# Fixed places for the plain matrix products of a fused attention and feed-forward kernel

## The chip, the core and the metric

The kernel runs on one core of a Trainium2 chip. A core has TensorE (matrix products, "PE" in the profile; its weight loads are "PEld"), VectorE ("DVE"), ScalarE ("ACT"), GpSimd ("POOL") and SyncE ("SP"), each with a queue of instructions of its own that it works through in order, and 16 DMA engines. Matrix products read SBUF and write PSUM. The metric is the time of one execution on the device in microseconds, lower is better.

## The reference

Inputs q, k, v have shape [8, 8, 576, 64]. Two attentions are added: a coarse one on means over groups of four tokens (144 by 144 scores), whose output is repeated four times, and a local one over a band of seven tokens. The sum, laid out as x of 4608 tokens by 512, goes through an RMS norm and a gated feed-forward layer of width 1536.

```python
def sm_attn(qq, kk, vv):                       # softmax(scale * qq kk^T) vv
q_d = q.reshape(B, H, S // 4, 4, D).mean(axis=3)       # k_d, v_d alike
out_up = np.repeat(sm_attn(q_d, k_d, v_d), 4, axis=2)
mask = np.abs(pos[:, None] - pos[None, :]) < 4         # local attention
x = (out_up + out_local) -> [4608, 512]
xn = x / np.sqrt(mean(x * x) + 1e-6) * rms_g
g, val = xn @ w_gate, xn @ w_val
out = (g / (1 + np.exp(-g)) * val) @ w_out
```

## The kernel before

**Chunks.** The tokens are worked in 18 chunks of 256, in two halves (`j`) of 128 partitions. A chunk's feed-forward layer has six inner tiles (`n` from 0 to 5), each of 256 columns of the inner width. Every product of this layer is made of three products of half-wide numbers in the type fp32r, because x, the weights and the inner values are each split into a high and a low part (`xh`, `xl`; `hs` holds both parts of the inner value).

- The *first products* (L1388, `ps_h<-xh,w` and `ps_h<-xl,w`, 128x256) are 24 for the gate and 24 for the value of an inner tile, 48 in all.
- Between them and the second products lie ScalarE's tanh (L1396, into `sil`), VectorE's gate step (L1399), VectorE's product with the value (L1404), ScalarE's high part (L1410, into `hs`) and VectorE's low part (L1413, into `hs`). "Gate or value steps" are L1399 and L1404, "an hs" is L1413.
- The *second products* (L1427, `ps_o<-wo,hs`, 128x512) are twelve for an inner tile. They are emitted one inner tile late (`LAG = 1`), behind the first products of the next inner tile, so that the second products of a chunk's last inner tile fall into the next chunk. `hs` has two buffers. Every third of the twelve reads the low part.

**Plain products.** Everything else on TensorE is in plain fp32 and writes one of three PSUM buffers named `ps_a`:

- for the coarse attention of two heads (one `Coarse` object, a "pair"): four products of scores (L593, "s"), then peaks and a scale on VectorE (L599, L608) and four exponentials on ScalarE (L613, into `a_g`), eight transposes of `a_g` ("turns", L623), two copies on ScalarE (L703), and eight products with the values (L638, "v"; each leaves two records in the trace, as the products of scores do), a scale into `o_g` on VectorE and a store to DRAM. The sums over four tokens that these need are made of loads by SP and POOL and additions (class `Sums`, L417);
- for a chunk's x: one product that sums the squares (L1010, "mean") and eight transposes of x (L1033, "x transposes"), after which ScalarE copies the high part xh (L1037) and VectorE subtracts to the low part xl (L1041).

**Local attention.** It is VectorE's and ScalarE's work, for the chunk that follows the one in the feed-forward layer: eight steps of score products (L917, `prod`, about 1 us each) and score sums (L921), a softmax, eight steps of value products (L970 on VectorE, L963 on ScalarE, a share on POOL) and value sums (L980 into `x_t`), two adds of the coarse output (L993), squares on ScalarE (L1003), the root of the norm, two scalings (L1020). The tile `x_t` has a limited number of buffers, so that the sums for one chunk wait until the x transposes of the chunk before have read the old contents.

**What sets the order.** Chunks 0 to 2, and the attention of the first chunks, are placed by a planner with a table of due times; the change leaves it alone. Chunks 3 to 17 run in a loop (L1571 to L1600). For each chunk it holds a list `todo` of pairs (time in half inner tiles, what to emit) for the next chunk: local attention, mean and x transposes from `Attention.steps`, and two pairs of heads from `Coarse.steps`. After each half inner tile it emits what is due:

```python
todo = nxt.steps(9.1 if c == FIRST else 6.5)
...
at = 1.2 + 2.5 * i
todo += zip((at + 0.1, at + 1.3), Coarse(*it).steps(lambda: fwd.last))
```

A scheduler of the language then orders what was emitted for each engine by its own estimate of when each instruction is ready; `tc.issue_after(x)` keeps an instruction behind `x` on its engine. Before the change only the products of scores (behind the last first product so far, `fwd.last`) and one first product of chunk 3 are pinned in this way. Twenty pairs of heads are done in this loop, two in each of the chunks 3 to 12; chunks 13 to 16 have only a mean and x transposes, chunk 17 nothing.

## Time and profile before

| what | value |
| --- | --- |
| median of 3 runs | 1089.92 us (1088.96 to 1090.8) |
| profiled execution | 1089.94 us, its span in the trace 1088.1 us |
| TensorE busy | 1066.7 us, 98% |
| TensorE weight loads busy | 970.2 us, 89% |
| VectorE busy | 909.6 us, 84% |
| ScalarE busy | 598.6 us, 55% |
| GpSimd busy | 160.8 us, 15% |

The span is the time from the first to the last record of the profiled execution; the rest of its time lies around it. Busy shares are averages over stages with different limits. The ends of matrix products in the trace are modelled, so where a product begins is read from its own start and where it ends from the start of the next one. A line of the timeline that joins several instructions ("x12") gives the start of the first.

### The profile page before, as it was taken

Reading aid. Unit: us, or ns where it says so; the run is one execution under the profiler, and the core shown is the slowest. Engines: PE = TensorE matmul, PEld = TensorE weight load, DVE = VectorE, ACT = ScalarE, POOL = GpSimd, SP = SyncE. Lnnn points to the kernel's source line nnn. Section 1 sums busy time; section 2 is a strip of 40 time slices with the busy share of each in tenths; the row PEclk is TensorE's granted clock in tenths of the full one; section 3 lists DMA queues with packets and bytes.
Section 4 is the critical chain, followed back from the end, with each engine's and each line's share of the span. In section 5 each row is a group of like instructions: output and inputs, shape, how many; then the busy total and the mean of one; then the engine's idle time right before and its main releaser. Section 6 shows DMA issues by size and latency. Waiting matters only on the chain.

```text
span 1088.1 us, 21642 instructions
## 1 busy us (share of the span) xinstructions
PE 1066.7 (98%) x7983; PEld 970.2 (89%) x7983; DVE 909.6 (84%) x1554; ACT 598.6 (55%) x2029; POOL 160.8 (15%) x200
## 2 busy tenths in 40 slices
PE   7899999999999999999999999999999999999997
PEld 4569899899989999999999999999999999999996
DVE  7799999798969897979797979798998898986421
ACT  4686565737266565656564737383737373645111
POOL 6544564300210101010101010100000000000000
PEclk9899999999999999999999999999999999999999
DMA  9885657333654535353525253522221222210000
GB/s 292 274 237 167 182 134 155 77 91 86 132 102 117 118 99 102 107 106 87 126 85 128 68 130 86 132 77 82 63 86 54 79 78 74 80 40 20 1 20 20
DMA packets 79182, 114.09 MB, mean 105 GB/s; under 512 B 33038, under 2 KB 40406, under 8 KB 79076
## 3 DMA queue, kind: packets, MB, share of 16 engines
q1 hardware_dynamic: 48308, 88.40, 26.3%
q0 software_dynamic: 11680, 19.78, 11.6%
q10 hardware_dynamic: 19088, 4.53, 1.9%
q8 instruction: 62, 1.02, 0.4%
q14 instruction: 44, 0.36, 0.1%
HBM read 100.86 MB, written 11.80 MB: 104 GB/s over the span
## 4 chain that ended last, share of the span: by engine, by line
PE 85%; DVE 6%; DMA 3%; issue 2%; POOL 2%; ACT 1%; SPq 1%; DVEq 0%; POOLq 0%; ACTq 0%
PE ps_h L1388 51%; PE ps_o L1427 25%; PE ps_a L638 3%; DMA w<-in_w_val_dram 1%; PE ps_a L593 1%; PE ps_a L623 1%; DVE prod L917 1%; PE ps_a L1033 1%; DVE x_t L980 1%; DVE sc L921 1%; PE ps_a L1258 1%; DVE sil L1404 0%; POOL hs L1413 0%; DMA vs<-in_v_sum_dram 0%; DMA wo<-in_w_val_dram 0%
## 5 line engine op out<-in xcount | busy, mean ns | idle before, releaser
L1388 PE MATMUL ps_h<-xh,w 128*128 128x256 f32 x3456 | 632.6, 281 | 0.0
L1388 PEld LDWEIGHTS ps_h<-xh,w 128*128 128x128 f32 x3456 | 537.6, 188 | 9.7 <-issue 3.1
L1388 PE MATMUL ps_h<-xl,w 128*128 128x256 f32 x1728 | 482.5, 280 | 0.0
L1427 PE MATMUL ps_o<-wo,hs 128*128 128x512 f32 x1296 | 327.1, 396 | 4.2 <-POOL hs L1413 1.7
L1388 PEld LDWEIGHTS ps_h<-xl,w 128*128 128x128 f32 x1728 | 325.2, 188 | 5.8 <-issue 2.0
L963 ACT ACTIVATE prod<-kv,sc 128x64 f32<-128x64 f32 x1024 | 261.9, 406 | 28.9 <-DVE sc L954 15.5
L1427 PEld LDWEIGHTS ps_o<-wo,hs 128*128 128x128 f32 x1296 | 232.8, 188 | 49.1 <-DVE hs L1413 2.8
L980 DVE TENSOR_REDUCE x_t<-prod 128x128 f32<-128x896 f32 x128 | 134.5, 1080 | 39.5 <-PE ps_a L1033 36.8
L1410 ACT ACTIVATE hs<-sil 128x512 fp32r<-128x512 f32 x108 | 68.2, 631 | 165.5 <-DVE sil L1404 140.1
L1396 ACT ACTIVATE sil<-ps_h 128x512 f32<-128x512 f32 x108 | 64.1, 595 | 148.7 <-PE ps_h L1388 140.8
L917 DVE TENSOR_TENSOR prod<-q_t,kv 128x896 f32<-128x896 f32 x128 | 138.6, 1089 | 0.2
L921 DVE TENSOR_REDUCE sc<-prod 128x14 f32<-128x896 f32 x128 | 136.9, 1075 | 0.2
L1399 DVE SCALAR_TENSOR_TENSOR sil<-sil,ps_h 128x512 f32<-128x512 f32 x108 | 73.7, 683 | 52.1 <-ACT sil L1396 52.1
L970 DVE TENSOR_TENSOR prod<-sc,kv 128x384 f32<-128x384 f32 (+1 forms) x128 | 105.9, 868 | 0.1
L1404 DVE SCALAR_TENSOR_TENSOR sil<-sil,ps_h 128x512 f32<-128x512 f32 x108 | 73.9, 684 | 22.6 <-PE ps_h L1388 22.1
L417 POOL DMA_DIRECT2D qk<-in_qk_sum_dram x42 | 39.0, 928 | 340.0 <-DMA qk<-in_qk_sum_dram 282.1
L1413 DVE TENSOR_TENSOR hs<-sil,hs 128x512 fp32r<-128x512 f32 x102 | 69.9, 685 | 17.9 <-ACT hs L1410 17.8
L613 ACT ACTIVATE a_g<-ps_a,m_g 72x144 f32<-72x144 f32 x128 | 46.5, 370 | 54.2 <-DVE m_g L608 50.0
L417 POOL DMA_DIRECT2D vs<-in_v_sum_dram x42 | 39.4, 937 | 104.1 <-DMA vs<-in_v_sum_dram 80.7
L1003 ACT ACTIVATE up_t<-x_t 128x128 f32<-128x128 f32 x128 | 39.1, 305 | 18.3 <-DVE x_t L993 12.2
L638 PEld LDWEIGHTS ps_a<-vs,a_g 72*72 72x72 f32 x512 | 39.2, 150 | 7.4 <-ACT a_g L613 2.9
L638 PE MATMUL ps_a<-vs,a_g 72*72 72x64 f32 x512 | 40.8, 234 | 5.1 <-ACT a_g L613 2.7
(154 smaller groups left out, 808.0 us busy)
## 6 DMA issues: line engine op xcount, KB each, us to landing
kv<-in_k_pad_dram SPq DMA_DIRECT2D x56, 320.0 KB
kv<-in_v_pad_dram SPq DMA_DIRECT2D x56, 320.0 KB
qk<-in_qk_sum_dram POOLq DMA_DIRECT2D x42, 288.0 KB, 4.5
out_dram<-o_sb SPq DMA_DIRECT2D x96, 72.0 KB
vs<-in_v_sum_dram POOLq DMA_DIRECT2D x42, 144.0 KB, 4.3
q_t<-in_q_band_dram SPq DMA_DIRECT2D x150, 36.0 KB
w<-in_w_gate_dram SPq DMA_DIRECT2D x8, 512.0 KB
w<-in_w_val_dram SPq DMA_DIRECT2D x8, 512.0 KB
```

The lines of the kernel that those rows point to most:

```text
L417: nc.gpsimd.dma_start(out=t, in_=(qk_sum, v_sum)[i][self.b, j, :, self.half], accum_op=ALU.add)
L638: nc.tensor.matmul(out=op[:, par, c], lhsT=at[:, kc, c * HALF:(c + 1) * HALF], rhs=self.sums.vs[:, 2 * (self.hp % 2) + par, kc], start=(kc ...
L917: nc.vector.tensor_tensor(out=pr, in0=bcast(q[:, s0:s0 + 2], 2, NO), in1=window(k, s0), op=ALU.mult)
L921: nc.vector.tensor_reduce(out=self.sc[:, j, par, s0:s0 + 2], in_=self.pr[i], axis=AX.X, op=ALU.add,)
L963: nc.scalar.activation(out=self.pr[i][:, o, s], in_=self.v[j, par][:, s0 + s + o], func=AF.Copy, scale=p[:, s, o:o + 1],)
L970: (nc.vector if engine == "DVE" else nc.gpsimd).tensor_tensor(out=self.pr[i][:, a:b], in0=bcast(p[:, :, a:b].rearrange("p s o -> p o s"), ...
L980: nc.vector.tensor_reduce(out=self.x[j][:, s0:s0 + 2, par], in_=pr.rearrange("p o s d -> p s d o"), axis=AX.X, op=ALU.add,)
L1388: self.last = nc.tensor.matmul(out=p[n][:, i], lhsT=wi[:, k], rhs=xi[:, k], start=(m == 0), stop=(m == 3 * KT - 1),).ins
L1399: nc.vector.scalar_tensor_tensor(out=self.sil[n], in0=self.sil[n], scalar=1.0, in1=self.g[n], op0=ALU.add, op1=ALU.mult,)
L1404: nc.vector.scalar_tensor_tensor(out=self.sil[n], in0=self.sil[n], scalar=0.5, in1=self.v[n], op0=ALU.mult, op1=ALU.mult,)
L1413: (nc.gpsimd if engine == "POOL" else nc.vector).tensor_tensor(out=self.hs[n][:, 1], in0=self.sil[n], in1=self.hs[n][:, 0], op=ALU.subtract,)
L1427: nc.tensor.matmul(out=self.o[j], lhsT=lhs[:, cols], rhs=rhs, start=(f == 0 and m == 0), stop=(f == NF - 1 and m == 2),)
```

## The change

In chunks 4 to 17 the plain products of the next chunk and of the coarse attention no longer come from `todo`. Each chunk has `slots`: lists of what to emit in inner tile `n`, behind its 48 first products and ahead of the twelve second products of inner tile `n - 1`. `in_line` chains these plain products and the second products behind one another on TensorE, beginning behind the last first product, and the next gate's first product is put behind the last of them. The slots are:

- 0: values of the second pair of the chunk before, scores of the first pair;
- 2: turns of the first pair, and the next chunk's mean with what follows it up to the norm;
- 3: values of the first pair, scores of the second;
- 4: the x transposes of the next chunk, with xh and xl;
- 5: turns of the second pair.

A pair's two turns are now emitted ahead of its two copies. The value steps of local attention are emitted 0.25 apart in place of 0.42, the adds at 4.1 and 4.9 in place of 4.8 and 6.4, and the loads of the next pair's sums in the chunk ahead, at 9.0 (`sum_up`). Chunk 3 keeps its `todo` list, without slots; its last second products fall into chunk 4 and are placed there.

```diff
@@ -508,6 +508,16 @@
     whole_og = {}
+    line = {"last": None}
+
+    def in_line(make):
+
+        with tc.issue_after(line["last"]) if line["last"] else nullcontext():
+            done = make()
+        if line["last"]:
+            line["last"] = done.ins
+        return done
+
     class Coarse:
@@ -538,6 +548,32 @@
                 self.store()
             return low, high
+
+        def sum_up(self):
+            if (self.b, self.hp // 2) not in sums:
+                sums[self.b, self.hp // 2] = Sums(self.b, self.hp // 2)
+            self.sums = sums[self.b, self.hp // 2]
+
+        def emit_scores(self):
+            self.sum_up()
+            self.scores()
+            self.peak(0)
+            self.peak(1)
+            self.scale()
+            self.powers(0)
+            self.powers(1)
+
+        def emit_turns(self):
+            self.invert()
+            for par in range(2):
+                self.turn(par)
+            for par in range(2):
+                self.copy(par)
+
+        def emit_values(self):
+            self.values()
+            self.scaled()
+            self.store()
         def plan(self, at, after=()):
             b, hp, tag = self.b, self.hp, self.tag
...
@@ -787,9 +823,19 @@
                 self.low(j)
             todo = [(0.37 * i, lambda i=i: score(i)) for i in range(8)] + [(3.0, softmax)]
-            todo += [(3.1 + 0.42 * i, lambda i=i: value(i)) for i in range(8)]
-            todo += [(at, lambda j=j: add(j)) for j, at in enumerate((4.8, 6.4))]
+            todo += [(3.1 + (0.42 if mean_at else 0.25) * i, lambda i=i: value(i)) for i in range(8)]
+            todo += [(at, lambda j=j: add(j)) for j, at in enumerate((4.8, 6.4) if mean_at else (4.1, 4.9))]
+            if mean_at is None:
+                self.emit_root = root
+                return todo
             return todo + [(mean_at, root), (10.4, lambda: turn(0)), (10.5, lambda: turn(1))]
+
+        def emit_x(self):
+            for j in range(2):
+                self.turn(j)
+            for j in range(2):
+                self.high(j)
+                self.low(j)
         def plan(self):
             c, np_, T = self.c, self.np, due[self.c]
...
@@ -1424,10 +1470,10 @@
             for j in range(2):
                 cols = slice(j * P, (j + 1) * P)
                 for m, (lhs, rhs) in enumerate(((hh, w[0]), (hh, w[1]), (hl, w[0]))):
-                    nc.tensor.matmul(
+                    in_line(lambda: nc.tensor.matmul(
                         out=self.o[j], lhsT=lhs[:, cols], rhs=rhs,
                         start=(f == 0 and m == 0), stop=(f == NF - 1 and m == 2),
-                    )
+                    ))
         def copy(self, j):
             if j == 0:
...
@@ -1568,25 +1614,48 @@
-    att, late = atts[FIRST], []
+    att, late, ahead, behind = atts[FIRST], [], [], None
     for c in range(FIRST, NCH):
-        todo = []
-        if c + 1 < NCH:
+        todo, slots = [], {}
+        n = min(2, len(coarse) - done)
+        pairs = [Coarse(*it) for it in coarse[done:done + n]]
+        done += n
+        if c == FIRST:
             nxt = Attention(c + 1, 4, 0)
-            todo = nxt.steps(9.1 if c == FIRST else 6.5)
-            n = min(2, len(coarse) - done)
-            for i, it in enumerate(coarse[done:done + n]):
+            todo = nxt.steps(9.1)
+            for i, it in enumerate(pairs):
                 at = 1.2 + 2.5 * i
-                todo += zip((at + 0.1, at + 1.3), Coarse(*it).steps(lambda: fwd.last))
-            done += n
-            todo.sort(key=lambda t: t[0])
+                todo += zip((at + 0.1, at + 1.3), it.steps(lambda: fwd.last))
+        else:
+            if behind:
+                slots[0] = [behind.emit_values]
+            behind = None
+            if pairs:
+                a, behind = pairs
+                slots.setdefault(0, []).append(a.emit_scores)
+                slots[2] = [a.emit_turns]
+                slots[3] = [a.emit_values, behind.emit_scores]
+                slots[5] = [behind.emit_turns]
+            if c + 1 < NCH:
+                nxt = Attention(c + 1, 4, 0)
+                todo = nxt.steps(None)
+                slots.setdefault(2, []).append(nxt.emit_root)
+                slots[4] = [nxt.emit_x]
+        if done < len(coarse):
+            todo.append((9.0, Coarse(*coarse[done]).sum_up))
+        todo.sort(key=lambda t: t[0])
         fwd = Forward(att)
         for n in range(NF // 2):
             for half in range(2):
-                if c == FIRST and half == 0 and n == NF // 2 - 1:
-                    fwd.behind = nxt.meant
+                if half == 0:
+                    fwd.behind = nxt.meant if c == FIRST and n == NF // 2 - 1 else line["last"]
+                    line["last"] = None
                 (fwd.emit_value if half else fwd.emit_gate)(n)
                 if half:
+                    if c > FIRST:
+                        line["last"] = fwd.last
+                    for emit in slots.get(n, []):
+                        emit()
                     late.append((fwd, n))
                     if len(late) > LAG:
                         fw, g = late.pop(0)
```

The pieces left out put `in_line` around the products of scores, turns, values, the mean and the x transposes, in the same way.

What moves is shown at three places. The names are those of the program; the numbers in them tell buffers and parts of weights apart.

The first place is TensorE in the third inner tile of a chunk with coarse work: the end of its first products, the turns of a pair, and the second products behind them. Before:

```order
L1388 MATMUL ps_h<-xl_5939,w_1_805 128x256
L623 MATMUL ps_a<-ident_sb,a_g 72x72
L1388 MATMUL ps_h<-xh_5938,w_1_806 128x256
L1388 MATMUL ps_h<-xh_5938,w_1_805 128x256
L1388 MATMUL ps_h<-xl_5939,w_1_805 128x256
L623 MATMUL ps_a<-ident_sb,a_g 72x72 x4
L1427 MATMUL ps_o<-wo_0_549,hs 128x512 x2
L623 MATMUL ps_a<-ident_sb,a_g 72x72 x3
L1427 MATMUL ps_o<-wo_0_549,hs 128x512
L1427 MATMUL ps_o<-wo_0_550,hs 128x512
```

After:

```order
L1434 MATMUL ps_h<-xl_4393,w_1_805 128x256
L1434 MATMUL ps_h<-xh_4392,w_1_806 128x256
L659 MATMUL ps_a<-ident_sb,a_g 72x72 x8
L1056 MATMUL ps_a<-ss,same_sb 128x8
L1473 MATMUL ps_o<-wo_0_549,hs 128x512
L1473 MATMUL ps_o<-wo_0_550,hs 128x512
L1473 MATMUL ps_o<-wo_0_549,hs 128x512 x2
```

The eight turns stood in three pieces among first and second products; now they stand in one piece, with the mean behind them, and only second products follow.

The second place is TensorE where chunk 3 ends and chunk 4 begins: the x transposes of chunk 4, its first first products, and the second products of chunk 3's last inner tile. Before:

```order
L1033 MATMUL ps_a<-ident_sb,x_t 128x128 x8
L1427 MATMUL ps_o<-wo_2_1329,hs 128x512
L1427 MATMUL ps_o<-wo_2_1330,hs 128x512
L1427 MATMUL ps_o<-wo_2_1329,hs 128x512
L1427 MATMUL ps_o<-wo_2_1330,hs 128x512
L1388 MATMUL ps_h<-xh_3717,w_0_359 128x256 x3
L1427 MATMUL ps_o<-wo_2_1329,hs 128x512 x3
L1427 MATMUL ps_o<-wo_2_1330,hs 128x512
L1427 MATMUL ps_o<-wo_2_1329,hs 128x512 x2
L1427 MATMUL ps_o<-wo_2_1330,hs 128x512
L1427 MATMUL ps_o<-wo_2_1329,hs 128x512
L1388 MATMUL ps_h<-xl_3718,w_0_359 128x256
```

After, in two pieces, between which stand the rest of the 48 first products:

```order
L1434 MATMUL ps_h<-xh_2882,w_2_906 128x256
L1079 MATMUL ps_a<-ident_sb,x_t 128x128 x8
L1434 MATMUL ps_h<-xh_3727,w_0_359 128x256 x2
L1434 MATMUL ps_h<-xl_3728,w_0_359 128x256
L1434 MATMUL ps_h<-xh_3727,w_0_360 128x256
L1434 MATMUL ps_h<-xh_3727,w_0_359 128x256
```

```order
L1434 MATMUL ps_h<-xl_3728,w_0_359 128x256
L1434 MATMUL ps_h<-xh_3727,w_0_360 128x256
L629 MATMUL ps_a<-qk 72x144 x4
L1473 MATMUL ps_o<-wo_2_1329,hs 128x512
L1473 MATMUL ps_o<-wo_2_1330,hs 128x512
L1473 MATMUL ps_o<-wo_2_1329,hs 128x512 x2
```

The twelve second products stood in front of the first product that reads xl; now they stand behind all 48 first products of chunk 4's first inner tile, with the products of scores ahead of them.

The third place is VectorE in chunk 13, from the second to the third hs after the x transposes. Before:

```order
L1413 TENSOR_TENSOR hs<-sil,hs 128x512
L1399 SCALAR_TENSOR_TENSOR sil<-sil,ps_h 128x512
L917 TENSOR_TENSOR prod<-q_t,kv 128x896
L921 TENSOR_REDUCE sc<-prod 128x14
L1404 SCALAR_TENSOR_TENSOR sil<-sil,ps_h 128x512
L921 TENSOR_REDUCE sc<-prod 128x14
L917 TENSOR_TENSOR prod<-q_t,kv 128x896
L1399 SCALAR_TENSOR_TENSOR sil<-sil,ps_h 128x512
L1413 TENSOR_TENSOR hs<-sil,hs 128x512
```

After:

```order
L1459 TENSOR_TENSOR hs<-sil,hs 128x512
L963 TENSOR_TENSOR prod<-q_t,kv 128x896
L1026 TENSOR_REDUCE x_t<-prod 128x2x64
L967 TENSOR_REDUCE sc<-prod 128x14
L1445 SCALAR_TENSOR_TENSOR sil<-sil,ps_h 128x512
L1039 TENSOR_TENSOR x_t<-x_t,up_t 128x512
L963 TENSOR_TENSOR prod<-q_t,kv 128x896 x2
L1450 SCALAR_TENSOR_TENSOR sil<-sil,ps_h 128x512
L967 TENSOR_REDUCE sc<-prod 128x14 x2
L1445 SCALAR_TENSOR_TENSOR sil<-sil,ps_h 128x512
L963 TENSOR_TENSOR prod<-q_t,kv 128x896
L1459 TENSOR_TENSOR hs<-sil,hs 128x512
```

Between the two there were two steps of score products and two of score sums; now there are four of the products, three of the sums, a value sum and an add.

## Rows read from the trace of the kernel before

**Rows 1.** Busy time by stretch, two stretches of 60 us. Columns: stretch, its length, then busy us and number of instructions of PE, PEld, DVE, ACT and POOL, the granted TensorE clock, the DMA share and GB/s.

```profile
280.00:340.00 60.00, 58.02 (x457) 52.77 (x456) 48.85 (x90) 31.62 (x123) 9.41 (x11) 1.00 0.56 124
580.00:640.00 60.00, 60.00 (x468) 55.77 (x468) 53.42 (x100) 33.15 (x119) 5.11 (x6) 1.00 0.42 99
```

**Rows 2.** The page's part on the chain that ended last: share of the span by engine, then by line.

```profile
PE 85%; DVE 6%; DMA 3%; issue 2%; POOL 2%; ACT 1%; SPq 1%; DVEq 0%; POOLq 0%; ACTq 0%
PE ps_h L1388 51%; PE ps_o L1427 25%; PE ps_a L638 3%; DMA w<-in_w_val_dram 1%; PE ps_a L593 1%; PE ps_a L623 1%; DVE prod L917 1%; PE ps_a L1033 1%; DVE x_t L980 1%; DVE sc L921 1%; PE ps_a L1258 1%; DVE sil L1404 0%; POOL hs L1413 0%; DMA vs<-in_v_sum_dram 0%; DMA wo<-in_w_val_dram 0%
```

**Rows 3.** The timeline of TensorE in one chunk with coarse work (560 to 611 us). Columns: start, duration of the group, engine, line, operation, output and inputs, shape, number.

```profile
561.65 0.28 PE L1388 MATMUL ps_h<-xh,w 128*128 128x256 f32 x1
...
562.71 0.41 PE L623 MATMUL ps_a<-ident_sb,a_g 72*72 72x72 f32 x4
562.93 0.71 PE L1427 MATMUL ps_o<-wo,hs 128*128 128x512 f32 x2
...
565.12 0.40 PE L1388 MATMUL ps_h<-xh,w 128*128 128x256 f32 x2
...
566.73 1.19 PE L638 MATMUL ps_a<-vs,a_g 72*72 72x64 f32 x16
567.86 0.71 PE L593 MATMUL ps_a<-qk 64*72 64x144 f32 x8
568.50 0.38 PE L1388 MATMUL ps_h<-xl,w 128*128 128x256 f32 x1
...
581.57 0.34 PE L1010 MATMUL ps_a<-ss,same_sb 128*128 128x8 f32 x2
581.76 3.01 PE L1427 MATMUL ps_o<-wo,hs 128*128 128x512 f32 x12
584.61 0.28 PE L1388 MATMUL ps_h<-xh,w 128*128 128x256 f32 x1
...
590.07 2.91 PE L1427 MATMUL ps_o<-wo,hs 128*128 128x512 f32 x12
592.82 0.28 PE L1388 MATMUL ps_h<-xh,w 128*128 128x256 f32 x1
...
595.57 1.04 PE L1033 MATMUL ps_a<-ident_sb,x_t 128*128 128x128 f32 x8
596.36 0.36 PE L1388 MATMUL ps_h<-xh,w 128*128 128x256 f32 x1
...
599.27 2.93 PE L1427 MATMUL ps_o<-wo,hs 128*128 128x512 f32 x12
602.04 0.40 PE L1388 MATMUL ps_h<-xh,w 128*128 128x256 f32 x2
...
607.69 2.93 PE L1427 MATMUL ps_o<-wo,hs 128*128 128x512 f32 x12
```

**Rows 4.** The timeline of TensorE in five short stretches: x transposes of chunks 5, 13 and 17, and the second products at two places of the last chunk (the number is cut by the end of the stretch; the start is what is read).

```profile
371.92 0.93 PE L1033 MATMUL ps_a<-ident_sb,x_t 128*128 128x128 f32 x7
...
819.41 0.82 PE L1033 MATMUL ps_a<-ident_sb,x_t 128*128 128x128 f32 x6
...
1023.26 0.82 PE L1033 MATMUL ps_a<-ident_sb,x_t 128*128 128x128 f32 x6
...
1035.09 0.39 PE L1427 MATMUL ps_o<-wo,hs 128*128 128x512 f32 x1
...
1067.94 0.62 PE L1427 MATMUL ps_o<-wo,hs 128*128 128x512 f32 x2
```

**Rows 5.** The timeline of TensorE, and below it that of VectorE, where chunk 4 begins (318 to 326 us). In brackets the idle time before a group and what ended it.

```profile
319.36 1.04 PE L1033 MATMUL ps_a<-ident_sb,x_t 128*128 128x128 f32 x8
321.17 1.19 PE L1427 MATMUL ps_o<-wo,hs 128*128 128x512 f32 x4 [0.77 <-ACT hs L1410]
...
323.49 2.13 PE L1427 MATMUL ps_o<-wo,hs 128*128 128x512 f32 x8 [0.78 <-DVE hs L1413]
325.46 0.28 PE L1388 MATMUL ps_h<-xl,w 128*128 128x256 f32 x1
...
324.09 0.70 DVE L1041 TENSOR_TENSOR xl<-ps_a,xh 128x512 fp32r<-128x512 f32 x1
```

**Rows 6.** The timeline of VectorE behind the x transposes of chunk 13 (818 to 848 us).

```profile
820.04 2.08 DVE L980 TENSOR_REDUCE x_t<-prod 128x128 f32<-128x896 f32 x2 [3.86 <-PE ps_a L1033]
822.04 0.68 DVE L1399 SCALAR_TENSOR_TENSOR sil<-sil,ps_h 128x512 f32<-128x512 f32 x1
822.64 1.28 DVE L1041 TENSOR_TENSOR xl<-ps_a,xh 128x512 fp32r<-128x512 f32 x2
823.83 1.72 DVE L970 TENSOR_TENSOR prod<-sc,kv 128x384 f32<-128x384 f32 x2
825.35 0.72 DVE L1404 SCALAR_TENSOR_TENSOR sil<-sil,ps_h 128x512 f32<-128x512 f32 x1
...
838.41 1.07 DVE L921 TENSOR_REDUCE sc<-prod 128x14 f32<-128x896 f32 x1
839.40 0.68 DVE L993 TENSOR_TENSOR x_t<-x_t,up_t 128x512 f32<-128x512 f32 x1
840.00 1.08 DVE L917 TENSOR_TENSOR prod<-q_t,kv 128x896 f32<-128x896 f32 x1
...
847.39 0.68 DVE L1413 TENSOR_TENSOR hs<-sil,hs 128x512 fp32r<-128x512 f32 x1
```

More of the change, by code (lines that the diff above doesn't have):

```diff
@@ L592, in scores @@
                     with tc.issue_after(last) if last else nullcontext():
-                        mm = nc.tensor.matmul(
+                        mm = in_line(lambda: nc.tensor.matmul(
                             out=self.s[par][:, c], lhsT=qs[rows, hp % 2, c * HALF:(c + 1) * HALF], rhs=ks[rows, hp % 2],
                             start=True, stop=True,
-                        )
+                        ))
                     last = mm.ins if self.behind else None
@@ L622, in turn @@
                 for c in range(2):
-                    nc.tensor.transpose(
+                    in_line(lambda: nc.tensor.transpose(
                         out=tp[:, kc, c * HALF:(c + 1) * HALF],
@@ L626, in turn @@
                         identity=ident_sb[:HALF, :HALF],
-                    )
+                    ))
         def copy(self, par, engine="ACT"):
@@ L637, in values @@
                     for kc in range(2):
-                        nc.tensor.matmul(
+                        in_line(lambda: nc.tensor.matmul(
                             out=op[:, par, c], lhsT=at[:, kc, c * HALF:(c + 1) * HALF],
                             rhs=self.sums.vs[:, 2 * (self.hp % 2) + par, kc], start=(kc == 0), stop=(kc == 1),
-                        )
+                        ))
         def invert(self):
@@ L1009, in mean @@
             self.rp = ps_a.tile([P, 2 * US], FP32, name="ps_a")
-            self.meant = nc.tensor.matmul(out=self.rp, lhsT=same_sb, rhs=self.ss, start=True, stop=True).ins
+            self.meant = in_line(lambda: nc.tensor.matmul(out=self.rp, lhsT=same_sb, rhs=self.ss, start=True, stop=True)).ins
         def rms(self):
@@ L1032, in turn @@
             for s in range(US):
-                nc.tensor.transpose(out=tp[:, s], in_=x[:, s], identity=ident_sb)
+                in_line(lambda: nc.tensor.transpose(out=tp[:, s], in_=x[:, s], identity=ident_sb))
             self.tp[j] = tp.rearrange("p s (r k) -> p k r s", k=KT)
@@ L1426, in second @@
                 for m, (lhs, rhs) in enumerate(((hh, w[0]), (hh, w[1]), (hl, w[0]))):
-                    nc.tensor.matmul(
+                    in_line(lambda: nc.tensor.matmul(
                         out=self.o[j], lhsT=lhs[:, cols], rhs=rhs,
                         start=(f == 0 and m == 0), stop=(f == NF - 1 and m == 2),
-                    )
+                    ))
         def copy(self, j):
@@ L1597, in attn_moe_kernel @@
         att = nxt
-    assert done == len(coarse)
+    assert done == len(coarse) and not behind
     for fw, g in late:
```

## The prediction

> **What bounds the kernel now.** I read first the busy time by stretch [rows 1]: from 340 us on TensorE is busy in 60.00 of 60 us, at a granted clock of 1.00, which is the 2.4 GHz level. Only the stretch 280 to 340 has a hole, 1.98 us, and the clock stayed at 1.00 through it, so a wait of that size costs itself and no more. The chain of waits says the same: 85% of it is TensorE, 76% the first and second products [rows 2]. So a change pays here only by shortening what TensorE does or by adding waits to it, and the rest of the reading is the timeline of TensorE by starts (ends are modelled, starts are not).
>
> What to see there [rows 3]: the same 48 first products take 5.46 us (584.61 to 590.07) in one place and 5.65 us (602.04 to 607.69) in another. That is 113.8 and 117.7 ns each, at the same clock. The quick stretch comes after v, m and then second products directly (581.76). The slow one comes after the x transposes followed directly by first products (596.36), where 24 take 2.91 us against 2.75 (592.82 to 595.57), and the twelve second products at 599.27 do not end the slow pace. So the pace of first products hangs on what stands behind a group of plain products.
>
> [...]
>
> **The change, part by part.** Gain first.
>
> 1. An inner tile without plain products. In the last chunk the starts of the twelve second products are 8.21 us apart ((1067.94 - 1035.09)/4) [rows 4]; six make 49.28 us.
>
> 2. The plain groups, each ending in second products [rows 3]. The exit from m into second products makes twelve of them 2.85 us (581.76 to 584.61) in place of 2.75 (590.07 to 592.82): 0.10 us, which I take for every group. No row shows an exit from scores into second products; bounds are 0 and 0.25, so 18 such exits may add 2.7 us or save 1.8.
>  - values and scores (v, s), twice in a chunk: 1.13 + 0.64 + 0.10 = 1.87 us each;
>  - turns and the mean: eight turns in one piece 0.50 (four start-to-start take 0.22, 562.71 to 562.93, rounded up), the mean 0.19, exit 0.10: 0.79 us;
>  - turns of the other pair: 0.60 us;
>  - the x transposes: 0.79 (595.57 to 596.36) + 0.10 = 0.89 us.
>  Sum 6.02 us; a chunk with coarse work is then 55.30 us.
>
> 3. Before, eight periods from x transposes to x transposes take (819.41 - 371.92)/8 = 55.94 us [rows 4]. The gain is 0.64 us a chunk. About 0.35 of it is pace (24 products at 2.91 for 2.75 and 48 at 5.65 for 5.46). The rest is turns that stood scattered: between 561.65 and 565.12 stand eight first products (8 x 0.114), eight second (8 x 0.229) and eight turns, 3.47 us, so the turns cost 0.73 us in place of 0.60, and each way in and out once more. Nine chunks (4 to 12): 5.8 us.
>
> 4. Chunks 13 to 16 have only the mean and the x transposes: 49.28 + 0.89 + 0.29 = 50.46 us against (1023.26 - 819.41)/4 = 50.96 [rows 4]. Four times 0.50: 2.0 us. Gain in all: 7.8 us.
>
> Now what it costs. The slots are fixed, so TensorE no longer takes whatever is ready.
>
> 5. From chunk 3 to 4. Before, behind the x transposes stand the twelve second products of chunk 3's last inner tile, and they fill the time until xl is there: x transposes at 319.36, second products at 321.17 and 323.49, first products from 325.46 [rows 5]. VectorE writes the second half of xl at 324.09 + 0.70 = 324.79. After, the 48 first products of chunk 4 come directly and all but the first two need xl. They can start at 324.8, 0.66 us earlier, with the twelve second products (2.75 us) still to do: 2.1 us lost. Bounds 0 and 2.75.
>
> 6. VectorE after the x transposes. Its sums into x_t wait for them (a buffer comes free): 819.41 to 820.04, 0.63 us [rows 4, 6]. From there to the third hs after, the new order has, in chunk 13 to 14, 33 instructions. By start-to-start of the rows: 8 sums x 1.00, 4 score products x 1.00, 3 score sums x 0.99, 6 value products x 0.76, 2 xl 1.19 together, 2 adds x 0.60, 6 gate or value steps x 0.60, 3 hs x 0.60: 27.3 us, and 0.1 for the end of the last. Before, one step more takes 820.04 to 847.39 + 0.68 = 28.0 us [rows 6], which fits. TensorE needs that hs in the third product of the fourth set of second products: 0.89 + 3 x 8.21 + 0.46 = 26.0 us after the x transposes begin. VectorE is there at 28.0: a wait of 2.0 us. Behind that hs in VectorE's queue stand the next steps, which come late too, but the debt is then paid, since TensorE has waited. The next chunk has two steps less before that hs (26.1 us of work): 0.8 us.
>
> 7. In the chunks with coarse work the same count is 27.3 us on VectorE (two steps less, but o_g, two peaks and a scale more, about 1.2 us), there at 28.0. TensorE takes longer, 26.0 + 0.60 + 1.87 = 28.5. So it fits by 0.5 us, where today TensorE never waits. Only chunk 4 to 5 has a gate step ahead of the sums that waits for ScalarE's tanh, some 1.3 us later, and one step more (0.6): 28.0 + 1.9 - 28.5 = 1.4, taken as 1.3 us.
>
> 8. The plain products themselves do not wait. Scores stand in slot 0, their turns two inner tiles (16.4 us) later, with two peaks, a scale and four exponentials between; x is added up by 839.40 + 0.68, 20.7 us after the transposes [rows 6], and the mean comes about 36 us after them. The loads of sums are issued earlier than before (in the chunk ahead, at 9.0 half tiles) on SP and POOL, which wait for nothing new. Cost 0. SP's other loads move with VectorE and ScalarE; that cover gone would show as VectorE waiting for kv, and costs within rival C.
>
> Waits: 2.1 + 1.3 + 2.0 + 0.8 = 6.2 us. Net 7.8 - 6.2 = 1.6 us faster. Against the profiled execution's 1089.94 us (span 1088.1; the median of the runs is 1089.92, so no correction) that is **1088.3 us**. Own range with the exits' bounds and half a microsecond either way on each of the four waits: 1084.5 to 1093.
>
> **The rivals.** Measurement can tell about 0.2% from no change, 2.2 us here: faster is below 1087.7, slower above 1092.1.
>
> A. The waits behind VectorE (steps 6, 7) do not come: VectorE or ScalarE gain some 2 us over the 28 because ScalarE's copies or the loads come at other moments. For it: the count rests on a stretch (831 to 836) in which products were a little dearer than elsewhere, and the margin is small. Against: VectorE has no idle time in those 28 us today [rows 6]. Time: 1089.9 - 7.8 + 2.1 = 1084.2.
>
> B. The pace does not come back: it is set by something else than what follows a plain group. Then only the scattered turns are saved, 0.29 x 9 = 2.6 us, and perhaps 0.4 in the last chunks, against 6.2 of waits: 1093.1. Against it speaks the place at 581.76 [rows 3]. [...]
>
> C. Slower: the margin of step 7 is eaten. One place, the third hs after the x transposes, in every coarse chunk, with VectorE as the engine that is late. It decides once VectorE needs 0.5 us (under 2%) more than my count from the x transposes to that hs. At 0.95 us more, eight chunks wait 0.45 and the other three places of steps 6 and 7 0.95 longer: 3.6 + 2.9 above the forecast, 1094.8. For it: fixed slots take away the freedom by which TensorE today runs second products in parts while it waits for hs. Against: before, the same count came out within 0.1 us of the row.
>
> D. The change does not do what it says (the scheduler still scatters the products). The order excludes it: turns now stand eight together in front of second products.
>
> **How the numbers follow.** Forecast 0.50, of it 0.22 below 1087.7 and 0.28 within. A 0.20, faster. B 0.10: 0.07 slower, 0.03 within. C 0.17: 0.14 slower, 0.03 within. What is left (exits dearer and waits smaller together, D) 0.03, within. Together faster 0.42, same 0.37, slower 0.21. The range 1083.0 to 1095.0 holds the forecast's own, most of A and the start of C.
>
> **What would show it.** Timeline of TensorE after: 48 first products at 5.46 us everywhere between chunks 5 and 16, none at 5.65; periods of x transposes at 55.3 and 50.5 us (right), or 55.6 and more without a wait (step 3 wrong, rival B). The waits list of TensorE should show second products waiting for VectorE's hs, about 4 us in three or four places and none in chunks 6 to 12, and first products waiting for xl once, about 4.4 us in all with what stood there before. VectorE's row of sums waiting for the x transposes should shrink from chunk to chunk. The forecast is wrong if TensorE waits in most coarse chunks (C), if it waits nowhere (A), or if scores into second products cost more than 0.25 us an exit.

## The result and the profile after

The changed kernel takes 1096.01 us (median of 6 runs, 1093.88 to 1098.19) against 1090.51 for the kernel before in the same runs: a ratio of 1.0054, 95% interval 1.0038 to 1.0070. It is slower, by about 0.5%. The profiled execution took 1095.53 us, its span is 1093.7 us.

The runs differ from one another ahead of chunk 4: over all runs told of here the x transposes of chunk 4 start between 316.60 and 324.34 us, although the programs are nearly the same up to there. So single runs are compared by the **rest**: the span less the start of chunk 4's x transposes. It is 768.74 us before (1088.1 - 319.36 [rows 5]) and 774.78 after (1093.7 - 318.92, below), 6.04 us more. (The expectations below speak of the time to the start of the last product instead, which is 6.7 to 6.9 us shorter.)

The list of TensorE's waits in the changed kernel from 318 to 1090 us (columns: who waits for whom, total us, times, longest):

```profile
PE ps_h L1434 <- DVE xl L1087: 2.6, 1, 2.6
PE ps_o L1473 <- DVE hs L1459: 1.8, 1, 1.8
PE ps_h L1434 <- ACT xh L1083: 1.2, 1, 1.2
```

5.6 us in three places, and none between chunks 5 and 13. Before, the same stretch had two waits of 0.8 [rows 5]. So waits are not the whole story. TensorE's timeline over one chunk with coarse work (the runs of 48 first products left out), which answers to [rows 3]:

```profile
592.19 1.03 PE L1079 MATMUL ps_a<-ident_sb,x_t 128*128 128x128 f32 x8
592.98 3.01 PE L1473 MATMUL ps_o<-wo,hs 128*128 128x512 f32 x12
601.29 0.67 PE L659 MATMUL ps_a<-ident_sb,a_g 72*72 72x72 f32 x8
601.76 3.01 PE L1473 MATMUL ps_o<-wo,hs 128*128 128x512 f32 x12
610.07 1.19 PE L674 MATMUL ps_a<-vs,a_g 72*72 72x64 f32 x16
611.19 0.71 PE L629 MATMUL ps_a<-qk 64*72 64x144 f32 x8
611.84 1.43 PE L1473 MATMUL ps_o<-wo,hs 128*128 128x512 f32 x5
...
620.35 2.93 PE L1473 MATMUL ps_o<-wo,hs 128*128 128x512 f32 x12
628.77 0.66 PE L659 MATMUL ps_a<-ident_sb,a_g 72*72 72x72 f32 x8
...
629.46 3.01 PE L1473 MATMUL ps_o<-wo,hs 128*128 128x512 f32 x12
637.77 1.19 PE L674 MATMUL ps_a<-vs,a_g 72*72 72x64 f32 x16
...
639.54 3.02 PE L1473 MATMUL ps_o<-wo,hs 128*128 128x512 f32 x12
648.06 1.03 PE L1079 MATMUL ps_a<-ident_sb,x_t 128*128 128x128 f32 x8
```

How to read the pace here: from the start of twelve second products to what follows the next 48 first products are 8.21 us at the quick pace and 8.42 at the slow one, and 0.10 more where a plain group stands ahead. Behind the x transposes (592.98 to 601.29) and behind the turns (601.76 to 610.07) it is 8.31: quick. Behind values and scores it is 8.51 (611.84 to 620.35), then 8.42: slow twice, until turns and mean (629.46 to 637.77, 8.31). Behind the second scores it is 8.52 again. So three of six stretches are slow, and a period is 648.06 - 592.19 = 55.87 us. In the whole kernel from 335 us on, 35 of 83 stretches of 48 first products are slow, at 5.65 us in place of 5.46.

### The profile page after: what moved, and what is told of

Read it like the earlier page. It is cut to its first block, busy times and chain, and to the rows that moved or that the text cites. A ratio compares the mean times of both kernels' runs of the same rounds, so it can differ in the third digit from the quotient of the medians.

```text
span 1093.7 us, 21627 instructions
## 1 busy us (share of the span) xinstructions
PE 1064.5 (97%) x7983; PEld 971.1 (89%) x7983; DVE 910.5 (83%) x1554; ACT 595.8 (54%) x2029; POOL 158.2 (14%) x200
## 4 chain that ended last, share of the span: by engine, by line
PE 84%; DVE 7%; DMA 3%; issue 2%; SPq 2%; POOL 1%; ACT 0%; DVEq 0%; POOLq 0%; ACTq 0%
PE ps_h L1434 50%; PE ps_o L1473 25%; PE ps_a L674 3%; PE ps_a L629 2%; SPq L309 1%; PE ps_a L659 1%; DVE prod L963 1%; DVE x_t L1026 1%; DMA w<-in_v_pad_dram 1%; PE ps_a L1079 1%; DVE sc L967 1%; DVE prod L1016 1%; DMA w<-in_qk_sum_dram 1%; DVE sil L1450 1%; DVE hs L1459 1%
## 5 line engine op out<-in xcount | busy, mean ns | idle before, releaser
L1434 PE MATMUL ps_h<-xh,w 128*128 128x256 f32 x3456 | 625.9, 280 | 1.2 <-ACT xh L1083 1.2
L1009 ACT ACTIVATE prod<-kv,sc 128x64 f32<-128x64 f32 x1024 | 264.8, 407 | 26.2 <-DVE sc L1000 14.9
L1459 DVE TENSOR_TENSOR hs<-sil,hs 128x512 fp32r<-128x512 f32 x102 | 70.0, 687 | 12.5 <-ACT hs L1456 12.4
```

The source lines that it names most:

```text
L1009: nc.scalar.activation(out=self.pr[i][:, o, s], in_=self.v[j, par][:, s0 + s + o], func=AF.Copy, scale=p[:, s, o:o + 1],)
L1434: self.last = nc.tensor.matmul(out=p[n][:, i], lhsT=wi[:, k], rhs=xi[:, k], start=(m == 0), stop=(m == 3 * KT - 1),).ins
L1459: (nc.gpsimd if engine == "POOL" else nc.vector).tensor_tensor(out=self.hs[n][:, 1], in0=self.sil[n], in1=self.hs[n][:, 0], op=ALU.subtract,)
```

## The experiments

All are single runs, but e9, whose row is the shortest of its six. They were taken in four sets (e1 to e4, e5 to e8, e9 and e10, e11 and e12), in which the kernel before took 1091.89, 1088.72, 1091.93 and 1095.24 us; so times of different sets are not to be compared as they stand. Rest, and its difference to the changed kernel's:

| run | time us | rest us | difference |
| --- | --- | --- | --- |
| kernel before (first profile) | 1089.94 | 768.74 | -6.04 |
| changed kernel | 1095.53 | 774.78 | 0 |
| e1 values last | 1093.54 | 770.91 | -3.87 |
| e2 scores behind | 1090.65 | 768.56 | -6.22 |
| e3 chunk 3's second products first | 1095.14 | 771.62 | -3.16 |
| e4 local scores held back | 1089.59 | 770.89 | -3.89 |
| e5 x transposes behind | 1097.78 | 772.99 | -1.79 |
| e6 e2, e3 and e4 | 1086.21 | 763.86 | -10.92 |
| e7 e1, e3 and e4 | 1085.94 | 763.85 | -10.93 |
| e8 e6, mean moved | 1084.30 | 762.96 | -11.82 |
| e9 e6, mean always behind | 1081.72 | 763.40 | -11.38 |
| e10 e9 with values last | 1086.17 | 763.42 | -11.36 |
| e11 e4, two means | 1095.86 | 773.47 | -1.31 |
| e12 e4, three means | 1103.02 | 776.86 | +2.08 |

One thing in this column belongs to no edit. In e1, e2, e4, e5, e11 and e12 TensorE stands idle at chunk 4 just as in the changed kernel (shown under e3), and its granted clock then falls to 0.50. Between 318 and 336 us the mean granted clock is 0.81 in the changed kernel, e5 and e11, but 0.91 in e1, e2, e4 and e12. From the x transposes of chunk 4 to the end of the next 48 first products it is 13.2 to 13.3 us in the first three and 12.3 to 12.4 in the other four. So about 0.9 us of the differences of e1, e2, e4 and e12 comes from a clock that was low for a shorter time.

**e1: scores first, then values.**

```diff
-            if behind:
-                slots[0] = [behind.emit_values]
-            behind = None
+            old, behind = behind, None
...
-                slots.setdefault(0, []).append(a.emit_scores)
+                slots[0] = [a.emit_scores]
...
-                slots[3] = [a.emit_values, behind.emit_scores]
+                slots[3] = [behind.emit_scores, a.emit_values]
...
+            if old:
+                slots.setdefault(0, []).append(old.emit_values)
```

> As the changed kernel (profiled execution 1095.53 us), but in the two slots that hold values and scores the scores stand first and the values directly in front of the second products. Theory 1 (the product that stands last in front of second products sets the pace of the first products, and scores set the slow one): no 48 first products at 5.65 us behind these slots, periods of x transposes 55.2 to 55.3 us in place of 55.87, about 5.4 us less, near 1090. Theory 2 (scores, the mean and x transposes each turn the pace over, quick to slow or slow to quick, wherever they stand in the group; turns and values leave it): periods stay at 55.87, near 1095.5.

The same products in another order inside the slot. TensorE's timeline:

```profile
665.51 0.71 PE L629 MATMUL ps_a<-qk 64*72 64x144 f32 x8
666.15 1.25 PE L674 MATMUL ps_a<-vs,a_g 72*72 72x64 f32 x16
667.21 3.01 PE L1473 MATMUL ps_o<-wo,hs 128*128 128x512 f32 x12
675.52 2.81 PE L1473 MATMUL ps_o<-wo,hs 128*128 128x512 f32 x11
```

667.21 to 675.52 is 8.31: quick. It is quick behind all 17 such groups, where the changed kernel was slow behind all 17; slow stretches fall from 35 to 11 of 83. The rest is 3.87 us shorter, less than the 5.4 of theory 1. The 24 slow stretches that are gone are 24 x 0.19 = 4.6 us and the shorter low clock at chunk 4 another 0.9; against them second products wait for hs in one chunk more (its period is 56.32 us, the others 55.31 to 55.62), 2.9 us in all in place of 1.8, and about half a microsecond is left unexplained. Theory 2 falls: the same groups, another pace.

**e2: values and scores behind the second products.**

```diff
-                    for emit in slots.get(n, []):
-                        emit()
+                    if n not in (0, 3):
+                        for emit in slots.get(n, []):
+                            emit()
...
                         fw.emit_second(g)
+                    if n in (0, 3):
+                        for emit in slots.get(n, []):
+                            emit()
```

> As the changed kernel, but values and scores stand behind the twelve second products of their slot, directly in front of the next first products. Theory 1 (the exit decides; in the kernel before, scores directly in front of first products were followed by the quick pace): quick first products everywhere, periods 55.2 to 55.4 us, near 1090.5. Theory 2 (scores turn the pace over wherever they stand): periods stay within 0.1 of 55.87, near 1095.5.

6.22 us less, and quick behind all these groups. So in two arrangements that share only this, that scores no longer stand directly in front of second products, the pace comes back. In both, 24 slow stretches are gone, and 24 x 0.19 = 4.6 us of the loss are pace; most of what remains of the 6.22 is the clock (0.9) and shorter waits for hs (1.3 us in place of 1.8). Left over in both are slow stretches behind the mean.

**e3: the cover at chunk 4 given back.**

```diff
+        if c == FIRST:
+            fw, g = late.pop(0)
+            fw.emit_second(g)
         assert not todo
```

> As the changed kernel, but the twelve second products of chunk 3's last inner tile are emitted ahead of chunk 4 again, so that they can run while xl is made. If the missing cover costs its wait alone (step 5 of the prediction): 2.1 us less, 1093.4. If the wait also lowers the granted clock (0.50 in the stretch 324 to 327 us of the changed kernel) and the first products behind it pay for that: 4.6 us less, 1090.9, and the granted clock stays at 1.00 between 318 and 333 us.

First the place in the changed kernel, TensorE's timeline, and busy time by stretch (columns as in [rows 1]):

```profile
318.92 1.04 PE L1079 MATMUL ps_a<-ident_sb,x_t 128*128 128x128 f32 x8
321.19 0.51 PE L1434 MATMUL ps_h<-xh,w 128*128 128x256 f32 x2 [1.24 <-ACT xh L1083]
324.32 0.58 PE L1434 MATMUL ps_h<-xl,w 128*128 128x256 f32 x1 [2.62 <-DVE xl L1087]
...
332.22 0.71 PE L629 MATMUL ps_a<-qk 64*72 64x144 f32 x8
```

```profile
322.60:329.40 6.80, 5.08 (x23) 5.08 (x24) 6.80 (x10) 5.86 (x26) 0.84 (x2) 0.50 0.72 133
324.00:327.00 3.00, 2.68 (x12) 2.68 (x13) 3.00 (x5) 2.06 (x10) 0.42 (x1) 0.50 0.63 99
327.00:330.00 3.00, 3.00 (x18) 3.00 (x17) 2.97 (x5) 3.00 (x14) 0.41 (x1) 0.60 0.58 145
330.00:333.00 3.00, 3.00 (x29) 2.68 (x28) 3.00 (x5) 3.00 (x14) 0.82 (x1) 1.00 0.47 96
```

TensorE is idle for 1.24 + 2.62 = 3.86 us, and from 322.6 to 329.4 us, so from within the second of these holes on, its granted clock is 0.50, the 1.2 GHz level (a stretch that the clock rises in shows a mean, as 0.60 from 327 to 330). From 327 us on 18 products stand in 3 us, where 26 would at 114 ns each. In the kernel before, the scores of the same tile stand at

```profile
330.78 0.71 PE L593 MATMUL ps_a<-qk 64*72 64x144 f32 x8
```

11.42 us behind the x transposes at 319.36 [rows 5]. That is 2.3 us more than x transposes, twelve second and 48 first products with their exit take (0.79 + 2.75 + 5.46 + 0.10 = 9.10). After, it is 13.30 us for the same without second products (6.35): 6.95 lost, 4.6 more than before. Of these 2.3 are idle time (3.86 against 0.77 + 0.78) and 2.3 the low clock. The Trainium skill, "TensorE: Matmul & The Clock Gate", section "Part 1: The HAM clock gate", says that an idle TensorE is put to half rate; these rows agree, 0.50 behind 3.86 us of idle time.

In e3 the same stretches:

```profile
324.00:327.00 3.00, 2.11 (x11) 1.61 (x10) 3.00 (x6) 3.00 (x14) 1.56 (x2) 1.00 0.53 67
327.00:330.00 3.00, 3.00 (x25) 2.92 (x24) 3.00 (x4) 2.89 (x12) 0.00 (x0) 1.00 0.70 122
```

The clock stays at 1.00 and the rest is 3.16 us shorter, between the two expectations. One inner tile later a new wait stands, on TensorE:

```profile
340.74 2.57 PE L1473 MATMUL ps_o<-wo,hs 128*128 128x512 f32 x10 [0.94 <-DVE hs L1459]
```

With it the two sum to 4.1, near the 4.6 of wait and clock together.

e3 shows something else, which bears on the theories above. From chunk 5's x transposes to chunk 17's its products on TensorE are the same, in the same order, as the changed kernel's. But its pace is not. TensorE's timeline of the same inner tiles as from 629.46 us on above:

```profile
628.92 3.01 PE L1473 MATMUL ps_o<-wo,hs 128*128 128x512 f32 x12
637.42 1.20 PE L674 MATMUL ps_a<-vs,a_g 72*72 72x64 f32 x16
...
639.19 3.02 PE L1473 MATMUL ps_o<-wo,hs 128*128 128x512 f32 x12
647.52 1.04 PE L1079 MATMUL ps_a<-ident_sb,x_t 128*128 128x128 f32 x8
```

8.50 behind turns and mean and 8.33 behind values and scores, where the changed kernel has 8.31 and 8.52. It is so in every other period: behind values and scores 4 of 17 stretches are quick in e3, behind turns and mean 4 of 9 are slow. So neither the kind of group in front of second products nor the order of products on TensorE decides alone.

**e4: VectorE's local scores held back in the last chunks.**

```diff
-                self.score(i)
+                with tc.issue_after(pin) if pin and i == 0 else nullcontext():
+                    self.score(i)
...
-                todo = nxt.steps(None)
+                todo = nxt.steps(None, lowed[c - 1, 0] if not pairs else None)
```

(`lowed` keeps the instruction that writes the low part of hs, by chunk and inner tile.)

> As the changed kernel, but in chunks 13 to 16 the local attention's score products are held on VectorE behind the hs of the chunk before's first inner tile, so that they no longer stand ahead of the third hs after the x transposes. If VectorE's order is what makes the second products wait there (step 6): no second products that wait for hs in the last chunks, 2.4 us less, 1093.1, periods near 51. If it is hs itself (ScalarE's part) or the loads: the two waits stay, 1095.5.

In the changed kernel, TensorE and VectorE at the wait of chunk 13 to 14 (x transposes at 868.15):

```profile
893.66 0.62 PE L1473 MATMUL ps_o<-wo,hs 128*128 128x512 f32 x2
896.05 2.56 PE L1473 MATMUL ps_o<-wo,hs 128*128 128x512 f32 x10 [1.77 <-DVE hs L1459]
...
946.91 3.30 PE L1473 MATMUL ps_o<-wo,hs 128*128 128x512 f32 x12
```

```profile
868.78 2.08 DVE L1026 TENSOR_REDUCE x_t<-prod 128x128 f32<-128x896 f32 x2 [0.53 <-PE ps_a L1079]
...
895.32 0.67 DVE L1459 TENSOR_TENSOR hs<-sil,hs 128x512 fp32r<-128x512 f32 x1
```

From the sums at 868.78 to the end of the third hs at 895.99 VectorE works without a hole, and the second products wait for it. In e4 TensorE waits nowhere behind 330 us, and the periods of the last chunks fall from 52.63, 51.80 and 50.80 to 50.79, 50.80 and 50.79, 2.85 us in all, more than the 2.2 of the waits because the pace behind them is another: from chunk 15's x transposes to chunk 16's five stretches are slow in the changed kernel and two in e4. The rest is 3.89 us shorter. The other 1.0 us is no effect of this edit: the stall at chunk 4 is the same there (1.2 + 2.6 us), but the clock was low for a shorter time, from 322.0 to 325.4 us (stretches of e4, whose x transposes start 2 us earlier):

```profile
322.00:325.30 3.30, 2.99 (x14) 2.99 (x15) 3.30 (x5) 2.36 (x11) 0.00 (x0) 0.50 0.81 144
325.40:330.00 4.60, 4.60 (x43) 4.28 (x42) 4.57 (x7) 4.60 (x20) 1.65 (x2) 1.00 0.44 99
```

So what one stall costs by the clock differs from run to run by about 1 us.

**e5: x transposes in front of first products.** The edit of e2, with inner tile 4 in place of 0 and 3.

> As the changed kernel, but the x transposes of the next chunk stand behind the second products of their slot, directly in front of first products. Theory 1 (the exit of a group of plain products sets the pace; x transposes directly into first products gave the slow one before the change): behind the x transposes first products at 5.65 us for 48, once in a chunk with coarse work and three times in the last chunks, 0.19 us each, 9 x 0.19 + 4 x 3 x 0.19 = 4 us more, less the two waits for hs (2.2 us), which go because x comes 2.75 us later: 1097. Theory 2 (place does not matter, only which groups there are): no more slow first products than in the changed kernel, 1093.3.

A miss for both theories, nearer to the second (2.2 us less). The time itself, 1097.78, is close to the first theory's 1097, but only because chunk 4 begins late in this run, at 322.71 us. The waits for hs go, the rest is 1.79 us shorter.

```profile
654.87 1.04 PE L1079 MATMUL ps_a<-ident_sb,x_t 128*128 128x128 f32 x8
661.20 0.66 PE L659 MATMUL ps_a<-ident_sb,a_g 72*72 72x72 f32 x8
```

6.33 us less 0.79 of x transposes is 5.54: quick. Of 13 such places 8 are quick and 5 slow. So it is not true that the exit from x transposes into first products sets the slow pace by itself, as the kernel before had made it seem.

**e6 and e7: the three edits together**, e4's in all chunks from 5 on; e7 with the order of e1 in place of the place of e2.

> As the changed kernel with three edits together: values and scores behind the second products (e2), chunk 3's last second products ahead of chunk 4 (e3), and the local score products held behind an hs (e4), here in all chunks from 5 on. If the three losses are separate: from the start of chunk 4's x transposes to the last product 768.1 - 6.4 - 3.3 - 1.7 = 756.7 us, against 762.1 in the kernel before, so some 5 us less than the kernel before, 1085. If the waits only move to another place when one of them is taken away: 760 or more, 1088 to 1091.

> As e6, but instead of moving values and scores behind the second products, the scores stand first and the values last in front of them (e1). Theory 1: as e6 within 1 us, 756.5 to 758 us from the start of chunk 4's x transposes to the last product. Theory 2 is out by e1; if the gain of e2 came from the place behind the second products and not from the exit, this one is 2 us longer than e6.

Rests of 763.86 and 763.85 are 757.1 and 757.0 to the last product, near the 756.7 of separate losses. Alone e2, e3 and e4 gave 6.22 + 3.16 + 3.89 = 13.27 us; with the shorter low clock of e2 and e4, which e3 takes away in any case, left out it is 11.4, against 10.92 together. Beside e3 and e4, e1 and e2 are worth the same.

**e8, e9, e10: where the mean stands.** In e8 it is first in slot 2 (`insert(0, nxt.emit_root)`), and behind the second products in the last chunks; in e9 behind them everywhere; e10 is e9 with the order of e1.

```diff
-                slots.setdefault(2, []).append(nxt.emit_root)
...
+                    if n == 2 and FIRST < c < NCH - 1:
+                        nxt.emit_root()
```

> As e6, but the mean stands ahead of the turns (so that turns stand in front of the second products), and in the last chunks behind the second products. Theory 1, with the mean as a second group whose exit into second products sets the slow pace: the slow first products that are left in e6 (two stretches in every other chunk with coarse work, two in each of the last four: 9 x 0.19 + 8 x 0.19 = 3 us) go, of which the exits of the means moved give back 0.1 us each: 2 us less than e6. If the mean does not set the pace: within 0.5 us of e6.

> As e8, but the mean stands behind the second products of its slot in every chunk from 4 on, directly in front of first products, and turns alone in front of the second products. So every exit is one that was followed by the quick pace in the runs so far (x transposes, turns into second products; scores, mean into first products). If an exit's effect belongs to the kind of exit: no slow 48 left behind slot 2, 8 x 0.19 = 1.5 us less than e8, near 754.7 us from the start of chunk 4's x transposes to the last product, 1083. If it is decided by the exact moment at which the group stands, other stretches turn slow in its place: 756 or more, 1084.5. Against the kernel before 0.5 to 0.65% faster.

> As e9, but scores and then values in front of the second products (as e1, e7) in place of values and scores behind them. By kind of exit: as e9 within 1 us (values into second products were followed by the quick pace in 17 of 17 in e1). By the exact moment: a stretch of slow first products in some chunks, 1 us or more longer.

e8 gains 0.90 us, not 2: in three of the last four chunks the slow stretches go, but behind mean and turns the stretch is slow in 8 of 9 places. In e9 every exit is of a kind that had mostly been quick (the mean into first products in three of four places of e8), and still (TensorE's timeline):

```profile
623.84 0.28 PE L1057 MATMUL ps_a<-ss,same_sb 128*128 128x8 f32 x2
629.72 2.96 PE L1474 MATMUL ps_o<-wo,hs 128*128 128x512 f32 x12
```

629.72 - 623.84 = 5.88, 0.15 of it the mean: 5.73, slow, in 8 of 9 chunks with turns, while the same mean in the last chunks is followed by the quick pace 4 times of 4. So the kind of exit does not decide either. e10 comes out as e9, 0.02 us apart in the rest, and values into second products are quick in all 17 places, as in e1 and e7.

e9 was run six times: 1084.61 us (median of 6) against 1091.93 for the kernel before in the same runs, ratio 0.9937, interval 0.9914 to 0.9959. It is faster than the kernel before, by about 0.6%, and so than the changed one, which was slower than the kernel before in runs of its own.

**e11 and e12: the same mean two and three times.**

```diff
-            self.meant = in_line(lambda: nc.tensor.matmul(out=self.rp, lhsT=same_sb, rhs=self.ss, start=True, stop=True)).ins
+            for _ in range(2):
+                self.meant = in_line(lambda: nc.tensor.matmul(out=self.rp, lhsT=same_sb, rhs=self.ss, start=True, stop=True)).ins
```

> As e4, but the product for the mean is issued twice in a row into the same place (the second gives the same numbers again), so that second products begin some tenths of a microsecond later and nothing else stands elsewhere. If the pace behind a mean belongs to the kind of group: the first products of the two inner tiles behind the mean stay at 5.65 us for 48 in each of chunks 13 to 16, periods there 50.8 + 0.1 to 0.2 us. If it is drawn by the exact moment at which second products begin: quick in some or all of them, 5.46 us, periods near 50.5 to 50.6.

> As e11 with the product issued three times. Kind of group: slow again in all of chunks 13 to 16, periods as e11 + 0.1 to 0.2 us. Exact moment: quick or slow, not foreseen, but the same in chunks 14 to 16, whose groups stand alike.

TensorE's timeline of e4 (one mean), e11 (two), e12 (three), in the same inner tiles of chunk 14:

```profile
898.81 0.28 PE L1057 MATMUL ps_a<-ss,same_sb 128*128 128x8 f32 x2
898.95 3.01 PE L1474 MATMUL ps_o<-wo,hs 128*128 128x512 f32 x12
907.45 2.93 PE L1474 MATMUL ps_o<-wo,hs 128*128 128x512 f32 x12
915.87 1.04 PE L1080 MATMUL ps_a<-ident_sb,x_t 128*128 128x128 f32 x8
```

```profile
905.40 0.51 PE L1058 MATMUL ps_a<-ss,same_sb 128*128 128x8 f32 x4
905.76 3.01 PE L1475 MATMUL ps_o<-wo,hs 128*128 128x512 f32 x12
914.07 2.91 PE L1475 MATMUL ps_o<-wo,hs 128*128 128x512 f32 x12
922.28 1.03 PE L1081 MATMUL ps_a<-ident_sb,x_t 128*128 128x128 f32 x8
```

```profile
910.90 0.73 PE L1058 MATMUL ps_a<-ss,same_sb 128*128 128x8 f32 x6
911.49 3.01 PE L1475 MATMUL ps_o<-wo,hs 128*128 128x512 f32 x12
919.98 2.93 PE L1475 MATMUL ps_o<-wo,hs 128*128 128x512 f32 x12
928.41 1.03 PE L1081 MATMUL ps_a<-ident_sb,x_t 128*128 128x128 f32 x8
```

8.50 and 8.42 with one mean, 8.31 and 8.21 with two, 8.49 and 8.43 with three: slow, quick, slow. It is so in all four of the last chunks with one and with two, and in three of four with three. With two, a period is 0.18 us shorter although there is more to do (50.62 against 50.80). The forecast that chunks 14 to 16 come out alike failed for e12, where chunk 15 is quick. In the chunks with coarse work, where the mean stands behind turns, one, two and three means are all followed by the quick pace, and each one more only adds 0.22 us to a period. Which product stands there is the same in all three; only their number, and with it the moment at which second products begin, differs. These runs don't tell number and moment apart; but number alone cannot be it, since in e3 the same number gave both paces.

## Why the prediction was wrong

Forecast was 1088.3 us, a kernel 1.6 us faster; measured was 1096.01, 5.5 us slower.

**The step that failed** is 2 with 3: that each plain group which ends in second products is followed by the quick pace. It was read from one place (581.76 [rows 3]), where the mean stood last; the mean last gave the slow pace in all four of the last chunks of e4. The sizes in step 2 hold: values and scores with their exit were priced at 1.87 and take 1.77 (637.77 to 639.54) plus 0.10, turns 0.47 in place of 0.50 (601.29 to 601.76), x transposes 0.79 as read. The period came out at 55.87 in place of 55.30, by three slow stretches of 0.19 and 0.02 for each set of second products in them. Rival B had this mechanism, in the sense that the pace does not come back, but not its reason, since it does come back behind half of the groups.

**Step 4**: 50.46 was forecast for a last chunk without waits; e4 shows 50.80, again two slow stretches.

**Step 5**: the idle time was right (2.1 forecast, 2.3 measured). What failed is a sentence ahead of it, that a wait of that size costs itself and no more: it was read from idle times of 0.77 and 0.78, and does not hold for 3.86. The low clock doubled the price (in e1, e2, e4 and e12, with the same idle time, it would have added about 1.4 us in place of 2.3).

**Step 6** was right: 28.0 us forecast from the x transposes to the end of the third hs, 27.8 measured (868.15 to 895.99); 2.0 and 0.8 us of waits forecast, 1.8 and about 0.4 measured (3.30 for twelve in place of 2.93). e4 shows that VectorE's order was the cause.

**Step 7**: the margin held (the third hs ends 27.9 us behind the x transposes of chunks 6 to 12 and is needed at 28.6), and no chunk from 6 to 12 waits, so rival C did not happen; that the time is close to the one that it gave is luck. The 1.3 us from chunk 4 to 5 did not come either. VectorE's timeline of the changed kernel has the third hs behind chunk 5's x transposes (368.69 us) at

```profile
395.75 0.72 DVE L1459 TENSOR_TENSOR hs<-sil,hs 128x512 fp32r<-128x512 f32 x1
```

so it ends 27.8 us behind them, where 29.9 was forecast, and second products need it 28.6 us behind them. Here the count of VectorE's work was 2.1 us too high; by which of its instructions is not shown. The 0.94 us of e3 are another wait, for an hs of chunk 4's first inner tile, which no step forecast.

**The sum**: -1.6 forecast, + 35 x 0.19 = 6.7 of pace, + 2.3 of clock, + 0.2 of idle time, - 1.3 and - 0.6 of waits that did not come: 5.7, against 6.04 measured.

## What to carry to other kernels

A gain that rests on a pace of TensorE has to be read from every place of that kind in the trace, not from one that shows the wanted one; here a single product more or less turned it, and so did another run-up to the same products. Fixed places in an engine's order take away its freedom to fill a wait, so each needs its own cover: count what the other engine still has to do up to that point, as step 6 did. A stall of some microseconds on TensorE is to be priced with the clock behind it.

## What the runs showed that was not expected

First products of one shape at one granted clock (1.00) have two steady paces, 113.8 and 117.8 ns. As a rule each lasts through the next inner tiles, second products included (228.8 and 230.9 ns from start to start), until the next group of plain products, and behind that group either can follow. In the changed kernel and e1 to e12 the pace changes in ten places with no plain group between: eight times behind second products that waited or were stretched, twice (880.33 us in e8, 948.48 in e12) behind nothing that the trace shows. Much of it repeats from run to run: behind values and scores 17 of 17 are slow in the changed kernel, e4, e11 and e12, behind scores and values 17 of 17 are quick in e1, e7 and e10, and in e11 it is quick where e4 was slow. But in e3 the changed kernel's own order has 13 of 17. Why the two paces exist, and what decides between them, stays open; so does how much of it changes between runs, since no program was traced twice. Which buffers the products use, and what loads and other engines do at that moment, was not tested.

The price of the same stall differs between runs: behind 1.24 + 2.62 us of idle time the granted clock is 0.50 from 322.6 to 329.4 us in the changed kernel, and only from 322.0 to 325.4 in e4.
